# Attention and a gated convolution in one fused kernel: a running sum over all key tiles, a shorter last key tile, 64-row masks, a new order

## The chip, the core and the metric

The kernel runs on one core of a Trainium2 chip. A core has a matrix engine (TensorE; PE in the profile, with its weight loads as PEld), a vector engine (DVE), a scalar engine (ACT), GpSimd (POOL) and a queue engine (SP) that here issues all DMA transfers. Each engine works through its own instructions in the order in which the program lists them; semaphores tie them together. The metric is the time of the whole program on the device, in microseconds; lower is better.

## What is computed

Eight batches of eight attention heads (576 rows, head width 64), and then a feed-forward part on the 512 joined columns:

```python
cum = np.cumsum(np.maximum(s, 0.0), axis=-1)
bias = -(cum[:, :, :, None] - cum[:, :, None, :])
scores = np.where(causal, -1e9, scale * q @ k.T + np.minimum(bias, 0.0))
attn = np.exp(scores - max(scores));  attn = attn / (attn.sum(-1) + 1e-9)
x = attn @ v                                  # heads side by side: 576 x 512
h = np.maximum(x @ w_in, 0.0)                 # 576 x 1024
gate = sigmoid(3-tap convolution of h along the rows)
out = (h * gate) @ w_out                      # 576 x 512
```

## The kernel before

**Attention.** Two heads are handled as one pair, 32 pairs, four to a batch. The two heads of a pair lie in partitions 0 to 63 and 64 to 127, so that their matmuls use 64 rows of the array each and run side by side. Operands are split into a high and a low part. For each pair there are these tasks, with the names that the planner gives them:

- `sh` (line 803): one product of every query row with the keys, in parts for the query tiles 0 to 4 (4 has 64 rows). DVE takes the row maxima from it (`mx`, lines 820 and 825). Tiles 0 to 3 need a causal mask there, which a fused add-and-maximum (line 825) adds; that operation is followed by a read of its accumulator. Tile 4's first part needs none and uses a plain maximum (line 820).
- `tn` (line 841): a 128x128 transpose of the maxima on TensorE; ACT copies the result, a DMA puts it into the operand `eq`.
- `sc` (line 884): the scores transposed, key tile by key tile (448 columns for key tile 1, 320, 192 and, for the last, 64), four steps each; ACT takes the exponential into `pt` (line 906).
- The causal mask of the scores: in the pairs 0 to 8 (`p < B0`) TensorE adds it with a 128x128 bf16 matmul per head and key tile (line 888); later POOL zeroes the triangle in `pt` (line 919).
- `ad` (line 962): from pair 9 on, DVE or POOL add up key tiles 1 (from its second 128 columns on) to 4.
- `sum` (line 997): the sums of the exponentials over the keys, by matmuls with `onehot`. Output row block q (144 columns) of a head goes to one of four groups of 32 columns of the array; the second head uses them in reversed order.
- `pv` (line 944): the product with v, in the same groups of 32 columns.

**Feed-forward.** `h` (line 1094) and `o` (line 1189) are matmuls over the whole array, 1536 each; ACT, DVE and POOL do the convolution, the gate and the split between them (lines 1105 to 1161).

**Order.** Every piece of work is a task with a due time; a planner plays them against assumed durations and writes the program in the order that results. From pair 9 on the tasks of neighbouring pairs stand in one unbroken burst on TensorE:

```python
ORDER = ("sh0", "sh1", "sh2", "sum", "pv", "sc0", "sh3", "sc1", "sc2", "sc3")
```

so that burst p holds `sum` and `pv` of pair p-1, `sc` of p and `sh` of p+1. Feed-forward matmuls and the transpose fill the time between bursts.

## Time and profile before

| | |
|---|---|
| Time, median of 3 runs (lowest to highest) | 812.44 us (810.75 to 814.55) |
| Span of the profiled execution, first to last instruction | 810.0 us |
| TensorE busy | 772.9 us, 95% of the span |
| VectorE busy | 596.5 us, 74% |
| ScalarE busy | 442.1 us, 55% |
| GpSimd busy | 311.6 us, 38% |

The profiled execution lists its span and no time of its own; the runs' median lies 2.4 us above that span. Matmuls are pipelined, so the time from one matmul's start to the next one's is what a matmul costs, not its own duration.

### The profile page before, as it was taken

How to read it: one execution, taken by the hardware profiler on the slowest of the kernel's cores; microseconds unless marked ns; L12 is line 12 of the kernel's file. 1: busy time of each engine (PE TensorE's matmuls, PEld its weight loads, DVE VectorE, ACT ScalarE, POOL GpSimd, SP SyncE). 2: the span in 40 equal slices, each digit the busy share in tenths (PEclk: the TensorE clock that was granted, in tenths of full speed). 3: DMA queues.
4: the chain of work that ended last, by engine and by line, in shares of the span. 5: the costliest groups of instructions: out<-in, count | busy, mean ns of one | idle time of the engine just before them, and what ended most of it. 6: DMA issues, size and time to landing. Idle time of an engine off the chain costs nothing.

```text
span 810.0 us, 21043 instructions
## 1 busy us (share of the span) xinstructions
PE 772.9 (95%) x8371; PEld 693.5 (86%) x8371; DVE 596.5 (74%) x1379; ACT 442.1 (55%) x982; POOL 311.6 (38%) x411
## 2 busy tenths in 40 slices
PE   2699998989999999999999999999999999999998
PEld 2576777779998999999998999999998999998997
DVE  8779778885577778777778778777777778734632
ACT  4364565637455645646555645646455645645633
POOL 7054452433334443443434443543434433422212
PEclk9999999999999999999999999999999999999999
DMA  7355433320213222122213222132213211111001
GB/s 221 122 161 153 134 100 95 120 89 19 82 46 87 77 82 75 46 90 74 82 45 91 73 82 75 46 92 72 83 45 92 72 54 44 44 42 41 16 23 37
DMA packets 49805, 63.24 MB, mean 78 GB/s; under 512 B 5679, under 2 KB 38767, under 8 KB 49647
## 3 DMA queue, kind: packets, MB, share of 16 engines
q1 hardware_dynamic: 49707, 61.91, 25.1%
q8 instruction: 65, 1.06, 0.5%
q14 instruction: 33, 0.27, 0.1%
HBM read 48.60 MB, written 13.04 MB: 76 GB/s over the span
## 4 chain that ended last, share of the span: by engine, by line
PE 87%; DVE 4%; ACT 2%; POOL 2%; DMA 2%; issue 2%; SPq 0%; ACTq 0%; DVEq 0%; POOLq 0%
PE ps L1189 25%; PE ps L1094 25%; PE ps L884 15%; PE pv L944 10%; PE ps L803 6%; PE ps L997 5%; ACT pt L906 1%; DMA ek<-bx 1%; DVE junk L825 1%; DVE ct L1131 1%; PE ps L888 1%; DMA rb<-ri_d 1%; DVE ct L612 0%; ACT s L756 0%; DVE ct L1119 0%
## 5 line engine op out<-in xcount | busy, mean ns | idle before, releaser
L1189 PE MATMUL ps<-u,wo 128*128 128x288 f32 x1536 | 218.0, 299 | 2.0 <-POOL u L1161 1.4
L1161 POOL TENSOR_TENSOR u<-ct,u 128x576 fp32r<-128x576 f32 x64 | 96.7, 1510 | 314.2 <-ACT u L1157 286.2
L1094 PE MATMUL ps<-x,wi 128*128 128x290 f32 x1536 | 215.9, 298 | 0.0
L1189 PEld LDWEIGHTS ps<-u,wo 128*128 128x128 f32 x1536 | 207.6, 188 | 4.7 <-POOL u L1161 1.9
L1094 PEld LDWEIGHTS ps<-x,wi 128*128 128x128 f32 x1536 | 209.1, 190 | 1.1
L906 ACT ACTIVATE pt<-ps,bias_sb 128x288 f32<-128x288 f32 (+4 forms) x384 | 153.5, 477 | 64.7 <-PE ps L884 64.3
L1131 DVE SCALAR_TENSOR_TENSOR ct<-ht,cw_sb,ct 128x288 f32<-128x288 f32 (+1 forms) x256 | 134.3, 525 | 71.7 <-ACT ct L1117 66.8
L825 DVE CUSTOM_DVE_ANT_0 junk<-ps,mask 128x448 bf16<-128x448 f32 (+3 forms) x256 | 108.3, 423 | 27.7 <-PE ps L803 3.5
L884 PE MATMUL ps<-s 64*128 64x288 f32 (+4 forms) x1152 | 125.1, 314 | 3.3 <-DVE r L825 2.5
L884 PEld LDWEIGHTS ps<-s 64*128 64x128 f32 x1152 | 101.7, 189 | 13.0 <-ACT pt L906 5.7
L1105 ACT ACTIVATE ht<-ps 128x289 f32<-128x289 f32 x128 | 52.7, 412 | 83.6 <-PE ps L1094 82.1
L944 PE MATMUL pv<-pt,v 128*32 128x448 f32 (+4 forms) x1536 | 96.0, 395 | 0.0
L919 POOL TENSOR_SCALAR_AFFINE_SELECT pt<-pt 128x128 f32<-128x128 f32 x230 | 67.3, 312 | 73.2 <-ACT pt L906 70.8
L760 POOL TENSOR_TENSOR s<-raw,s 128x1152 fp32r<-128x1152 f32 x31 | 86.5, 2790 | 15.3 <-ACT s L756 9.6
L944 PEld LDWEIGHTS pv<-pt,v 128*32 128x32 f32 x1536 | 54.9, 111 | 38.0 <-issue 29.8
L884 PE MATMUL ps<-eq,ek 64*128 64x288 f32 (+4 forms) x384 | 74.4, 325 | 0.0
L803 PE MATMUL ps<-s 64*128 64x288 f32 (+4 forms) x384 | 66.5, 331 | 6.0 <-DVE r L820 3.2
L1117 ACT ACTIVATE ct<-ht,cw_sb 128x288 f32<-128x288 f32 x126 | 67.7, 537 | 5.8
L1206 ACT COPY ob<-ps 128x288 f32<-128x288 f32 x63 | 25.0, 397 | 80.5 <-PE ps L1189 68.1
L1150 DVE TENSOR_TENSOR ct<-ct,ht 128x576 f32<-128x576 f32 x64 | 54.4, 851 | 16.7 <-ACT ct L1144 16.7
L803 PE MATMUL ps<-ek,eb 64*128 64x288 f32 (+4 forms) x384 | 58.2, 320 | 6.4 <-DMA ek<-bx 6.4
L1144 ACT ACTIVATE ct<-ct 128x576 f32<-128x576 f32 x64 | 43.6, 681 | 31.5 <-DVE ct L1131 31.2
(87 smaller groups left out, 802.8 us busy)
## 6 DMA issues: line engine op xcount, KB each, us to landing
raw<-qk SPq DMA_DIRECT2D x32, 576.0 KB
v<-vp SPq DMA_DIRECT2D x32, 320.0 KB
rb<-ri_d SPq DMA_DIRECT2D x64, 144.0 KB
outT<-ob SPq DMA_DIRECT2D x64, 144.0 KB
ht<-w_out SPq DMA_DIRECT2D x16, 256.0 KB
w<-w_in SPq DMA_DIRECT2D x8, 512.0 KB
ri_d<-ri SPq DMA_DIRECT2D x32, 72.0 KB
rows_d<-bx SPq DMA_DIRECT2D x1, 1215.0 KB
```

The costliest lines, as they stand in the source:

```text
L760: tt_on(e)(st[:, 0:2, :], R_t[raw.slot], st[:, 2:4, :].bitcast(F32), op=ALU.subtract)
L803: nc.tensor.matmul(dst[j], l, m, start=(k == 0), stop=(k == 1))
L825: nc.vector.tensor_tensor_reduce(out=junk[:, 0 : c1 - c0], in0=bank(pb, o, o + c1 - c0), in1=mask[:, S - w + c0 : S - w + c1], scale=1.0, ...
L884: nc.tensor.matmul(dst[j], l, m, start=(k == 0), stop=(k == 3))
L906: nc.scalar.activation(PT_t[pts[j].slot][0:jt, O_T[t] + c0 : O_T[t] + c1], bank(pb, o, o + c1 - c0)[0:jt], AF.Sigmoid, bias=bias_sb[0:jt, ...
L919: nc.gpsimd.affine_select(out=reg, in_=reg, pattern=[[1, dg]], compare_op=ALU.is_ge, fill=0.0, base=0, channel_multiplier=-1,)
L944: nc.tensor.matmul(pvt[gs, o0 : o0 + c1 - c0], vt[0:jt, t, gs], PT_t[pts[g // 2].slot][0:jt, O_T[t] + c0 : O_T[t] + c1], start=(t == 0), s ...
L1094: nc.tensor.matmul(bank(hb, 0, XW), l, r, start=(k == 0), stop=(k == len(seq) - 1))
L1117: nc.scalar.activation(o, src, AF.Copy, scale=w)
L1131: nc.vector.scalar_tensor_tensor(cc[:, lo:hi], h_[:, sh + lo : sh + hi], cw_sb[:, 3 * f + k : 3 * f + k + 1], cc[:, lo:hi], op0=ALU.mult, ...
L1161: tt_on(e)(uu[:, 1], C_t[ct.slot], uu[:, 0].bitcast(F32), op=ALU.subtract)
L1189: nc.tensor.matmul(bank(pb, 0, HS), l, r, start=(fp == 0 and k == 0), stop=(fp == NF // 2 - 1 and k == len(seq) - 1),)
```

## The change

Five things change, and the planner's result with them.

- **Sum.** The running sum now covers all five key tiles: `ad` starts with key tile 1 added to tile 0's columns from 128 on (448 wide), and takes in tiles 2, 3 and 4 as before. The `sum` matmuls read tile 0's first 128 columns and `ad` alone, first all of one head, then all of the other.
- **Last key tile.** Its score matmuls load 66 weight columns where they loaded 128.
- **Early mask.** In pairs 0 to 8 the mask is added by bf16 matmuls of 64 rows and 64 columns, the two heads side by side. It is now also added to `sh`, and DVE takes the plain maximum there for all tiles.
- **Small ones.** The reciprocal is taken in place, the mask operands share `ad`'s memory, and the second pair's `dr` load no longer waits for the first one's in the plan.
- **Order.** The planner's matmul cost is now the larger of streaming and weight load, and every task's due time is shifted by a number from a table (`DUE`, 500 entries; two lines stand here).

```diff
+DUE = {
...
+    "tn":
+        "0 -7.46 2 15.64 3 12.43 4 -45.28 5 9.39 6 3.16 7 29 8 38.87 9 18.73 10 -5.31 11 28.45 "
...
-    unit = const.tile([P, P], BF16, name="unit")
+    unit = const.tile([P, D], BF16, name="unit")
-    ad_t = const.tile([P, 2, W_T[2]], F32, name="ad")
+    ad_t = const.tile([P, 2, W_T[1]], F32, name="ad")
+    mrow = ad_t.bitcast(BF16).rearrange("p a c -> p (a c)")[:, 0 : 4 * P].rearrange(
+        "p (k i m) -> p k i m", k=2, i=2
+    )
...
-        nc.gpsimd.tensor_copy(unit, ident)
+        nc.gpsimd.tensor_tensor(unit, ident[:, 0:D], ident[:, D:P], op=ALU.add)
+        nc.gpsimd.memset(mrow, 0.0)
+        for j in range(2):
+            for i in range(2):
...
-    def c_rt(n):
-        return n * 0.461e-3
+    def c_rt(part, last=P):
+        return sum(max((c1 - c0) / 2.4e3 + 0.013, 0.107 if t < L else last / 1.2e3)
+                   for t, c0, c1 in part)
...
                     for k in range(2):
+                        if k and p < B0 and tau < L:
+                            for i_ in range(0 if tau else 1, 2):
+                                for j, r in enumerate(lanes):
+                                    d0 = c1 - c0 - D * (2 - i_)
+                                    nc.tensor.matmul(
+                                        dst[j][:, d0 : d0 + D], mrow[r, 1, i_], unit[r],
+                                        start=False, stop=False,
+                                    )
...
+                    def plain(tau, c0):
+                        return c0 == 0 and (tau == L or p < B0)
-                        if tau == L and c0 == 0:
+                        if plain(tau, c0):
...
-                    ks = slice(P * t, P * t + P)
-                    dst = [bank(pb, o, o + cn) for pb in pbs]
+                    kn = min(P, J_T[t] + 2)
+                    dst = [bank(pb, o, o + cn)[0:kn] for pb in pbs]
...
-                                l = st[r, kk * S + P * t : kk * S + P * t + P]
+                                l = st[r, kk * S + P * t : kk * S + P * t + kn]
...
                             dg = min(P, cn)
-                            for j in range(2):
-                                nc.tensor.matmul(
-                                    dst[j][:, 0:dg], mask[:, S - P : S], unit[:, 0:dg],
-                                    start=False, stop=False,
-                                )
+                            for i_ in range(dg // D):
+                                for j, r in enumerate(lanes):
+                                    nc.tensor.matmul(
+                                        dst[j][:, D * i_ : D * i_ + D], mrow[r, 0, i_, 0:kn], unit[r],
+                                        start=False, stop=False,
+                                    )
...
-                for t in range(2, NT):
+                for t in range(1, NT):
...
-                            acc, pt[:, O_T[1] + P : O_T[1] + W_T[1]] if t == 2 else acc,
+                            acc, pt[:, P:S] if t == 1 else acc,
                             pt[:, O_T[t] : O_T[t] + W_T[t]], op=ALU.add,
...
                     rows.append([
-                        (0, pt[:, 0:S]), (P, pt[:, O_T[1] : O_T[1] + P]), (2 * P, ad_t[:, j, :])
+                        (0, pt[:, 0:P]), (P, ad_t[:, j, :])
                     ])
...
+            steps = [(i, j) for i in range(n) for j in range(2)]
+            if ad:
+                steps = [(i, j) for j in range(2) for i in range(n)]
...
-            nc.vector.reciprocal(ri_t, rs_t)
+            nc.vector.reciprocal(rs_t, rs_t)
...
+    for t in sch.tasks:
+        t.tag += shift.get(due(t.name), 0.0)
```

What this does to the program shows in the listed order. On TensorE, here is the sum of the fourth burst that has a running sum (pair 12); `pt0` and `pt1` are the two heads' exponentials, `ad` the running sum. Before:

```order
L803 MATMUL ps5_70<-ek2_86,eb_89 128x64
L997 MATMUL ps1_66<-pt0_92,onehot_74 32x144 x4
L997 MATMUL ps1_66<-pt1_93,onehot_74 32x144 x4
L997 MATMUL ps1_66<-pt0_92,onehot_74 32x16
L997 MATMUL ps1_66<-pt0_92,onehot_74 32x112
L997 MATMUL ps1_66<-pt1_93,onehot_74 32x16
L997 MATMUL ps1_66<-pt1_93,onehot_74 32x112
L997 MATMUL ps1_66<-ad_97,onehot_74 32x32
L997 MATMUL ps1_66<-ad_97,onehot_74 32x144 x2
L944 MATMUL pv_64<-pt0_92,v0_90 32x128 x2
```

and the same place after the change:

```order
L934 MATMUL ps5_70<-ek2_86,eb_89 128x64
L1136 MATMUL ps0_65<-pt0_92,onehot_74 32x128
L1136 MATMUL ps0_65<-ad_97,onehot_74 32x16
L1136 MATMUL ps0_65<-ad_97,onehot_74 32x144 x3
L1136 MATMUL ps0_65<-pt1_93,onehot_74 32x128
L1136 MATMUL ps0_65<-ad_97,onehot_74 32x16
L1136 MATMUL ps0_65<-ad_97,onehot_74 32x144 x3
L1082 MATMUL pv_64<-pt0_92,v0_90 32x128 x2
```

Eighteen matmuls became ten (the two `ad` rows of before stand once more, for the second head), and 2048 output columns became 1152. The order is now head by head.

The end of the same burst on TensorE, the last two score matmuls and what follows. Before, six feed-forward matmuls (`u`, `wo`) stand ahead of the transpose of the maxima (`ident`):

```order
L884 MATMUL ps0_65<-eq0_87,ek1_85 128x192
L884 MATMUL ps3_68<-eq0_87,ek1_85 128x192
L1189 MATMUL ps1_66<-u2_977,wo_79 128x288 x6
L841 MATMUL ps2_67<-ident_71,r0_98 128x128
L1189 MATMUL ps1_66<-u3_978,wo_79 128x288 x6
```

After:

```order
L1019 MATMUL ps2_67<-eq0_87,ek1_85 128x192
L1019 MATMUL ps4_69<-eq0_87,ek1_85 128x192
L976 MATMUL ps3_68<-ident_71,r0_98 128x128
L1328 MATMUL ps0_65<-u2_1189,wo_79 128x288 x6
L1328 MATMUL ps0_65<-u3_1190,wo_79 128x288 x6
```

The transpose now stands directly behind the burst. Of the 22 transposes from the first running sum on, that was so for 1 before and is so for 13 now; the others have six or more matmuls in between.

DVE behind that burst, where the running sum of pair 13 is made (`ad`; `ct` is the convolution, `rb` and `x` the normalized output). Before:

```order
L756 CAST s1_83<-raw1_81 128x1152
L962 TENSOR_TENSOR ad_97<-pt0_92 128x320
L1043 TENSOR_TENSOR rb_96<-pv_64,rb_96 128x576
L1058 CAST x_95<-rb_96 128x2x290
L962 TENSOR_TENSOR ad_97<-ad_97,pt0_92 128x64
L1062 TENSOR_TENSOR x_95<-rb_96,x_95 128x2x290
L962 TENSOR_TENSOR ad_97<-pt1_93 128x320
```

After:

```order
L879 CAST s0_82<-raw0_80 128x1152
L1099 TENSOR_TENSOR ad_97<-pt0_92 128x448
L1099 TENSOR_TENSOR ad_97<-ad_97,pt0_92 128x320
L1099 TENSOR_TENSOR ad_97<-pt1_93 128x448
L1099 TENSOR_TENSOR ad_97<-ad_97,pt0_92 128x192
```

The 448-wide add is new, and DVE makes nearly all adds itself: over the program it has 44 of the 46 adds of 448, and 43 of the 46 of 192 where it had 23.

## Rows read from the trace of the kernel before

**Rows 1.** Profile page, its first part: busy time, share of the span, instructions.
```profile
span 810.0 us, 21043 instructions
PE 772.9 (95%) x8371; PEld 693.5 (86%) x8371; DVE 596.5 (74%) x1379; ACT 442.1 (55%) x982; POOL 311.6 (38%) x411
```

**Rows 2.** Busy time by stretch: stretch, length, PE, PEld, DVE, ACT, POOL, clock, DMA.
```profile
25.00:200.00 175.00, 163.71 (x1855) 130.12 (x1854) 141.19 (x357) 95.94 (x221) 65.56 (x45) 0.97 0.36 111
200.00:700.00 500.00, 499.47 (x5572) 458.75 (x5570) 387.37 (x889) 282.38 (x635) 206.78 (x304) 1.00 0.23 70
700.00:810.00 110.00, 104.15 (x917) 99.96 (x917) 48.41 (x91) 54.17 (x114) 24.90 (x34) 0.99 0.11 35
```

**Rows 3.** The chain that ended last, 200 to 700 us, shares by line.
```profile
by line: PE ps L1094 29.0%; PE ps L1189 28.7%; PE ps L884 16.8%; PE pv L944 12.0%; PE ps L803 7.6%; PE ps L997 4.9%; PE ps L841 0.5%; ACT pt L906 0.5%; issue 0.1%; PE ps L888 0.0%
```

**Rows 4.** Timeline of PE in one burst: start, length, engine, line, operation, form, count.
```profile
303.44 0.79 PE L997 MATMUL ps<-pt,onehot 128*32 128x144 f32 x22
304.04 0.29 PE L997 MATMUL ps<-ad,onehot 128*32 128x144 f32 x1
304.06 0.27 PE L997 MATMUL ps<-pt,onehot 128*32 128x112 f32 x2
...
304.41 0.30 PE L944 MATMUL pv<-pt,v 128*32 128x128 f32 x1
...
307.26 0.67 PE L884 MATMUL ps<-s 64*128 64x288 f32 x6
...
307.89 0.31 PE L803 MATMUL ps<-s 64*128 64x320 f32 x2
...
308.39 0.98 PE L884 MATMUL ps<-s 64*128 64x288 f32 x6
...
310.02 0.46 PE L884 MATMUL ps<-s 64*128 64x64 f32 x5
...
310.54 0.53 PE L884 MATMUL ps<-s 64*128 64x320 f32 x4
...
311.73 1.06 PE L1189 MATMUL ps<-u,wo 128*128 128x288 f32 x6
312.63 0.27 PE L841 MATMUL ps<-ident,r 128*128 128x128 f32 x1
```

**Rows 5.** PEld by line and form: count, busy us, mean ns, idle before.
```profile
L884 PEld LDWEIGHTS ps<-s 64*128 64x128 f32 x1152 | 101.7, 189 | 13.0 <-ACT pt L906 5.7 <-DVE r L825 3.6 <-issue 0.5
L944 PEld LDWEIGHTS pv<-pt,v 128*32 128x32 f32 x1536 | 54.9, 111 | 38.0 <-issue 29.8
L888 PEld LDWEIGHTS <-mask 128*128 128x128 bf16 x90 | 5.2, 99 | 7.8 <-issue 6.6
```

**Rows 6.** Timeline of PE, an early pair.
```profile
59.74 1.77 PE L997 MATMUL ps<-pt,onehot 128*32 128x144 f32 x54
61.30 0.30 PE L944 MATMUL pv<-pt,v 128*32 128x128 f32 x2
...
64.19 0.66 PE L884 MATMUL ps<-s 64*128 64x288 f32 x6
...
69.65 0.33 PE L841 MATMUL ps<-ident,r 128*128 128x128 f32 x1
```

**Rows 7.** DVE by line and form, columns as in Rows 5.
```profile
L825 DVE DVE_READ_ACCUMULATOR2_ANT r<- 128x1 f32 x320 | 26.6, 83 | 0.0
L962 DVE TENSOR_TENSOR ad<-pt 128x320 f32<-128x320 f32 x41 | 24.8, 605 | 20.8 <-POOL pt L919 20.8
```

**Rows 8.** Waits, 0 to 200 us: who, for whom, total us, times, longest.
```profile
PEld ps L803 <- DVE r L820: 5.3, 9, 2.0
```

**Rows 9.** Timeline of DVE in the burst of Rows 4.
```profile
311.21 0.08 DVE L825 DVE_READ_ACCUMULATOR2_ANT r<- 128x1 f32 x1
```

**Rows 10.** Timeline of PE, second pair's first products.
```profile
24.58 0.75 PE L803 MATMUL ps<-ek,eb 64*128 64x288 f32 x2 [5.11 <-DMA ek<-bx]
```

More of the change, by code (lines that the diff above doesn't have):

```diff
@@ L3 @@
 import math
+import re
 from contextlib import ExitStack
@@ L60, with due @@
 ORDER = ("sh0", "sh1", "sh2", "sum", "pv", "sc0", "sh3", "sc1", "sc2", "sc3")
+KINDS = {
+    "sh": ("mx",), "tn": ("rt", "ds"), "sc": ("ex", "mk", "ad"), "pv": ("sum",),
+    "nm": ("gd", "inv", "ri", "rb", "xh", "xl"), "g": ("re", "ce", "ta", "ga", "mu", "uh", "ul"),
+    "o": ("oe", "st"),
+}
+DUE = {
+    "x":
+        "s -20.88 masks -12.84 ident -1.96 eb 25.43 cum 47.26 rows_d 1.9 rest 67.91 bias_cp 3.09 "
+        "cw -0.02 cwq 22.44 cwh 8.24",
+    "pads":
+        "0 -16.34 1 15.9 2 -14.42",
+    "ind":
[78 rows of a table added]
+}
+def due(name):
+    kind, rest = re.match(r"([a-z]+)(.*)", name).groups()
+    if not rest or kind in ("bias", "rows"):
+        return "x:" + name
+    for of, kinds in KINDS.items():
+        if kind in kinds:
+            kind = of
+    n = 2 if kind in ("h", "g", "o", "wo") else 1
+    return kind + ":" + ".".join(re.findall(r"^[\d.]*", rest)[0].split(".")[:n])
 class Buf:
@@ L350 @@
     cw_sb = const.tile([P, NF * 3], F32, name="cw_sb")
-    junk = const.tile([P, S], BF16, name="junk")
+    junk = const.tile([P, W_T[1]], BF16, name="junk")
     wi = const.tile([P, 2, NC, DF], F32R, name="wi")
@@ L371 @@
     rs_t = const.tile([P, RS], F32, name="rs")
-    ri_t = const.tile([P, RS], F32, name="ri")
     H_t = [const.tile([P, 2, XW], F32, name=f"ht{i}") for i in range(NHT)]
@@ L806, in pair @@
             w = sum(c1 - c0 for _, c0, c1 in part)
-            t_mm = add(f"sh{p}.{i}", [("PE", 2 * c_rt(w))], [t_hi, t_dr, t_eb],
+            t_mm = add(f"sh{p}.{i}", [("PE", 2 * c_rt([(0, *x[1:]) for x in part]) + (0 if p >= B0 else 0.06 * sum(2 if tau else 1 for tau, _, _ in part if tau < L)))],
+                       [t_hi, t_dr, t_eb, t_ident],
                        a_sh + 0.1 * i, sh_mm, alloc=pbs + ([r8] if i == 0 else []),
@@ L832, in pair @@
                     maxima.append(
-                        add(f"mx{p}.{j}.{tau}.{c0}", [("DVE", (0.15 if tau == L and c0 == 0 else 0.22) + (c1 - c0) / 0.96e3)],
+                        add(f"mx{p}.{j}.{tau}.{c0}", [("DVE", (0.15 if plain(tau, c0) else 0.22) + (c1 - c0) / 0.96e3)],
                             [t_mm, t_ident] + ([maxima[j]] if c0 else []), a_sh + 0.1 * i,
@@ L886, in sc_mm @@
                             dg = min(P, cn)
[L887 to L891 removed]
+                            for i_ in range(dg // D):
[3 more added lines that the diff above has]
+                                        start=False, stop=False,
+                                    )
                     o += cn
             w = sum(c1 - c0 for _, c0, c1 in part)
[L895 removed]
+            t_sc = add(f"sc{p}.{i}", [("PE", 4 * c_rt(part, 66) + (0 if p >= B0 else 0.06 * sum(-(-min(P, c1 - c0) // D) for _, c0, c1 in part if c0 == 0)))], [t_ident, t_shift, t_lo], A + 0.1 * i,
                        sc_mm, alloc=pbs + (pts if i == 0 else []), uses=[sb, ek, eq], mode="r",
@@ L969, in pair @@
                         f"ad{p}.{j}.{t}", [("DVE", c_tt(w), True, ADD_), ("POOL", c_pool(w), True, ADP)],
-                        [m for t_, m in masks[j] if t_ in (1, t)] + [t_ad], A + 2, pre_add,
-                        alloc=[ad] if (j, t) == (0, 2) else [], uses=[*pts] + ([] if (j, t) == (0, 2) else [ad]),
+                        [m for t_, m in masks[j] if t_ in (t - (t == 1), t)] + [t_ad] + last_mask, A + 2, pre_add,
+                        alloc=[ad] if (j, t) == (0, 1) else [], uses=[*pts] + ([] if (j, t) == (0, 1) else [ad]),
                     )
@@ L986, in sums @@
             n = len(rows[0])
-            for i in range(n):
-                for j in range(2):
-                    c0, src = rows[j][i]
-                    c1 = c0 + src.shape[1]
-                    for q in range(c0 // RS, 4):
-                        g = 3 - q if j else q
-                        a_, b_ = max(c0, q * RS), min(c1, (q + 1) * RS)
-                        if a_ >= b_:
-                            continue
-                        o0 = a_ - q * RS
-                        nc.tensor.matmul(
-                            bank(sb_, o0, o0 + b_ - a_)[32 * g : 32 * g + 32], onehot[:, j, :],
-                            src[:, a_ - c0 : b_ - c0], start=i == 0 and j == 0,
-                            stop=i == n - 1, tile_position=(0, 32 * g),
-                            skip_group_check=True,
-                        )
+            steps = [(i, j) for i in range(n) for j in range(2)]
+            if ad:
+                steps = [(i, j) for j in range(2) for i in range(n)]
+            for i, j in steps:
+                c0, src = rows[j][i]
+                c1 = c0 + src.shape[1]
+                for q in range(c0 // RS, 4):
+                    g = 3 - q if j else q
+                    a_, b_ = max(c0, q * RS), min(c1, (q + 1) * RS)
+                    if a_ >= b_:
+                        continue
+                    o0 = a_ - q * RS
+                    nc.tensor.matmul(
+                        bank(sb_, o0, o0 + b_ - a_)[32 * g : 32 * g + 32], onehot[:, j, :],
+                        src[:, a_ - c0 : b_ - c0], start=j == 0 and (i == 0 or (ad is not None and q > 0)),
+                        stop=j == 1 if ad else i == n - 1, tile_position=(0, 32 * g),
+                        skip_group_check=True,
+                    )
         ta = A1 + 1
         tq = ta - TQA
-        t_sum = add(f"sum{p}", [("PE", 1.0 if ad else 1.4)], [t_ident] + added + [m for t, m in masks[0] + masks[1]], tq, sums,
+        t_sum = add(f"sum{p}", [("PE", 0.6 if ad else 1.4)], [t_ident] + added + [m for t, m in masks[0] + masks[1]], tq, sums,
                     alloc=[sb_], uses=[*pts] + ([ad] if ad else []), mode="c32", burst=group(p + 1))
@@ L1238, in stay_awake @@
         )
+    shift = {
+        f"{kind}:{n}": float(v)
+        for kind, text in DUE.items() for n, v in zip(text.split()[::2], text.split()[1::2])
+    }
+    for t in sch.tasks:
+        t.tag += shift.get(due(t.name), 0.0)
     order = sch.play(
```

22 lines of the change are left out of this document (16 added, 6 removed), and 76 rows, old and new, of the table DUE.

## The prediction

> **What bounds the kernel now.** I read the page first: over 810.0 us TensorE is busy for 95%, the next engine, DVE, for 74% [rows 1]. A share is an average over stages, so the stretches come next. From 25 to 200 us TensorE works 163.7 of 175 us; from 200 to 700 us it works 499.5 of 500; in the last 110 us 104.2 [rows 2]. The chain says the same for the middle: 99.4% of it lies on seven matmul lines, 0.5% on ScalarE [rows 3]. The reader is to see that in these 500 us nothing but matmul time counts: what TensorE is spared there comes off the span, as long as no other engine then makes it wait. DVE is the one to watch: 387.4 of 500 us [rows 2]. Before 200 us TensorE is idle for 11.3 us, and waits there are mostly for DVE's row maxima: one line's weight loads wait 5.3 us for them [rows 8].
>
> **The sum.** One sum of before starts at 303.44 and the next task at 304.41: 0.97 us [rows 4]. Per head, tile 0 fills output columns 0 to 575, tile 1 128 to 255, `ad` 256 to 575. Counted over both heads (the second uses the groups in reversed order), the middle two of the four column groups carry 144+144+112+32+144 = 576 columns, the outer two 448. If the groups run side by side, a column costs 0.97/576 = 1.68 ns. The early sums check it: 800 columns in every group, 1.56 us [rows 6], 1.95 ns a column with many short pieces. After the change every group carries 288 columns: two blocks of 144, or 128+16 and 144. That gives 0.48 to 0.56 us; I take 0.50, since there are few short pieces. Saving 0.47 x 23 pairs = **10.8 us**. Bounds: nothing (first rival) to 11.3.
>
> Whether groups run side by side decides this, and the trace shows it. At 304.04 a matmul of `ad` starts, before the two 112-column ones of tile 1 that start at 304.06 and stand ahead of it in the program for either head [rows 4]. So a group goes on while another is behind. The Trainium skill, page "TensorE: Matmul & The Clock Gate", Part 3, "The mechanism", says the opposite: matmuls start and end strictly in program order, only weight loads are pulled ahead. By that rule the new order, 128 and 16 columns into one group ahead of the other three, would save nothing here (the first rival's 803.4 us). The trace contradicts it; the measurement decides.
>
> **The last key tile.** Its eight matmuls start at 310.02 and the next tile's last lane at 310.54, where 64 columns of streaming cannot be what takes 0.13 us a step: the weight loads are [rows 4]. A load of 128 columns shows 189 ns, one of 32 shows 111: 0.81 ns a column [rows 5]. 62 columns fewer are 50 ns. Of four loads the first lies under the 448-wide matmul before it, so three count (the two heads load side by side): 0.15 us a pair, x 32 = **4.8 us**. Bounds: 0 to 4 x 0.05 x 32 = 6.4.
>
> **The early mask.** A masked pair's scores take from 64.19 to 69.65, 5.46 us [rows 6]; an unmasked one's 307.26 to 307.89 and 308.39 to 311.73, 3.97 us [rows 4]. So ten full-array mask matmuls, with the array's tiling changed ten times, cost 1.49 us. They go. In come 9 steps of two 64-row matmuls in `sc` (two for each of four tiles, one for the last) and 7 in `sh`. No row has such a step. Below, 64 columns at the full clock are 27 ns; above, a step that waits for a whole fp32 weight load costs the 0.13 us just seen. The mask's bf16 loads are short, 99 ns against 189 [rows 5], so I stay near the low end: 0.05. Per pair -1.49 + 16 x 0.05 = -0.69, x 9 = **6.2 us** saved. Bounds: 16 x 0.13 = 2.08 would cost 5.3; 0.03 would save 9.1.
>
> DVE's maxima of the early pairs lose 72 accumulator reads (320 to 248 in the listed program) of 83 ns [rows 7], 6.0 us of DVE work; the plain maximum itself I cost like the fused one. It counts only where TensorE waits for maxima, at least the 5.3 us of [rows 8]; I take a third, **2 us**. Bounds 0 and 6.
>
> **More work for the running sum.** 46 adds of 448 columns: 320 take 605 ns [rows 7], so 0.6 to 0.85 us, near 0.75. DVE also takes over 20 adds of 192 from POOL. About 45 us more, less some casts and splits it hands to ACT and POOL. Spread over the middle stretch that is 387 + 40 of 485 us, 88%. It lies beside the matmuls and is costed at nothing there. Queued behind it on DVE are the convolution taps, which feed the gate, and the next maxima; the sum itself waits for the second head's last add. With the cover gone, each add that falls on the path would cost its 0.6 to 0.85 us.
>
> **The order.** Outside the early masks the array's tiling changes 146 times, 137 before, counted in the listed programs. A change costs at most 1.49/10 = 0.15 us, since the mask matmuls share that: **+1.4 us**, 0 as the other bound. 13 transposes now stand directly behind their burst. In the burst shown DVE's last maximum ended at 311.29 [rows 9], the burst at 311.73, and six matmuls of 0.90 us covered the rest before 312.63 [rows 4]. The burst gets 0.47 + 0.15 = 0.62 us shorter, so the maxima, if they end as they did, are 0.18 us late at a transpose without cover: **+2.6 us** for 13 with the 0.2 I take. What is behind a late transpose is the `eq` transfer for the next burst's scores, a whole stretch of feed-forward matmuls away.
>
> **The start.** The second pair's products waited 5.11 us, until 24.58, for their bias rows [rows 10]. That transfer now stands ahead of two 576 KB loads instead of behind one; but POOL first builds eight more mask pieces, ahead of the padding that this transfer waits for, and the first weight pieces stand on DVE between the second pair's maxima. I take zero, from -3 to +5 (the wait gone by half, or as long again). The in-place reciprocal, smaller tiles and the dropped plan edge are nothing: the buffer was already held until the spread was done.
>
> **Sum.** -10.8 - 4.8 - 6.2 - 2.0 + 1.4 + 2.6 = -19.8. From the span of 810.0 that is 790.2 us; the runs' median lies 2.4 above the span, and I leave that: **792.6 us**.
>
> **Rivals.**
>
> 1. *The sums do not speed up*, because a group's work blocks the others in the queue. Per head 144 columns in the outer group, then 144 in the others: 288 x 1.68 ns = 0.48, two heads 0.97, as now. For it: the new order puts four passes of one group first. Against: the starts at 304.04 and 304.06 [rows 4]. Time 792.6 + 10.8 = 803.4 us. Chance 0.07.
>
> 2. *Late maxima take the place of the removed work, and it gets slower.* Place: the transposes behind the burst, and the burst's own `sh` banks, which DVE must empty. Price: every 0.1 us by which DVE is later costs 2.2 us over 22 bursts. For it: DVE goes from 77% towards 88% in the middle, and the plan's durations only have to be wrong by a few per cent. Against: DVE still has 12% to spare, and before the plan met its marks to 0.5 us in 500. With 0.7 us more a burst it is 792.6 + 15.4 = 808.0; slower than before by over 0.5% it is from (816.5 - 792.6)/22 = 1.1 us a burst on, one and a half of the new adds in each. Chance of a loss of 0.5 us or more a burst 0.12, a quarter of it beyond 1.1.
>
> 3. *The early part gains nothing or loses*: the new mask steps cost as fp32 loads, the start takes 5 us more, the clock (granted at 0.97 there [rows 2]) drops once or twice more. 792.6 + 6.2 + 5.3 = 804.1 with the mask at its bound. Chance 0.09.
>
> The change not doing what it says would need 66 columns to load as slowly as 128: 797.4, inside the range.
>
> **Numbers.** The forecast, that TensorE's removed time comes off, has 0.72 (its own range 783 to 800); 0.07, 0.12 and 0.09 go to the rivals. To hold 8 in 10 the range takes in the first and most of the third rival: **782 to 804**. A measurement of this kernel can hardly tell a change under 0.5%, 4 us, from none. Faster by more than that (under 808.4): 0.72 + 0.07 + 0.09 + half of the second rival = 0.93, rounded to 0.92; within 0.5%: 0.04; slower: 0.04.
>
> **What would show it.** Right: a sum of about 0.5 us between `sh` and `pv` in the middle, and 23 of them; the last key tile's eight matmuls in about 0.37 us; an early pair's scores near 4.4 us; TensorE still over 99% busy in the middle stretch, which ends some 16 us earlier. Wrong: sums near 0.97 us; idle time ahead of the transpose with DVE's maximum named; waits for `ad`; a first score matmul later than before. The prediction fails if the middle is no longer all matmul time.

## The result, and the profile after

The changed kernel takes 789.5 us (median of four runs, 788.2 to 791.3) where the kernel before took 812.9 beside it: a ratio of 0.972, 95% interval 0.969 to 0.974. The prediction was 792.6 us, 782 to 804. The profiled execution's span fell from 810.0 to 788.0 us, by 22.0 where the sum of the terms said 19.8.

The page's first part and the middle stretch (columns as in [rows 1, 2]):

```profile
PE 744.9 (95%) x8201; PEld 669.6 (85%) x8201; DVE 595.3 (76%) x1375; ACT 439.2 (56%) x972; POOL 323.4 (41%) x408
```
```profile
200.00:700.00 500.00, 494.86 (x5324) 447.11 (x5317) 399.08 (x958) 288.70 (x645) 218.45 (x310) 1.00 0.23 70
```

TensorE's busy time fell by 28 us, the span by 22. The middle is no longer all matmul time: 494.9 of 500 us, where it was 499.5. The chain of 200 to 700 us says so as well; DVE and ScalarE stand on it now, against 0.5% of ScalarE alone in [rows 3]:

```profile
by line: PE ps L1233 27.9%; PE ps L1328 27.5%; PE ps L1019 16.6%; PE pv L1082 11.4%; PE ps L934 6.8%; PE ps L1136 2.7%; DVE ad L1099 1.1%; DVE ct L1270 1.1%; issue 0.9%; DVE junk L960 0.9%; PE ps L976 0.8%; DVE r L955 0.6%; ACT pt L1044 0.5
```

The timeline of TensorE in the burst of [rows 4], which now stands 12.4 us earlier:

```profile
291.00 0.30 PE L1136 MATMUL ps<-pt,onehot 128*32 128x128 f32 x1
291.01 0.32 PE L1136 MATMUL ps<-ad,onehot 128*32 128x144 f32 x3
...
291.57 2.87 PE L1082 MATMUL pv<-pt,v 128*32 128x128 f32 x48
...
296.93 0.31 PE L1019 MATMUL ps<-s 64*66 64x64 f32 x3
...
297.34 0.53 PE L1019 MATMUL ps<-s 64*128 64x320 f32 x4
...
298.51 0.33 PE L976 MATMUL ps<-ident,r 128*128 128x128 f32 x1
298.60 1.83 PE L1328 MATMUL ps<-u,wo 128*128 128x288 f32 x12
```

The sum takes 0.57 us (291.00 to 291.57) where it took 0.97; the last key tile 0.41 (296.93 to 297.34) where it took 0.52; the transpose behind the burst 0.09 until the next matmul. An `ad` matmul starts 0.01 us behind the 128-column one of another group. The early pair of [rows 6], in the same view:

```profile
61.65 0.23 PE L923 MATMUL ps<-unit,ad 64*128 64x64 bf16 x4
61.72 0.34 PE L934 MATMUL ps<-ek,eb 64*128 64x192 f32 x2
61.89 0.59 PE L1019 MATMUL ps<-s 64*128 64x288 f32 x6
...
66.21 0.33 PE L976 MATMUL ps<-ident,r 128*128 128x128 f32 x1
```

Four mask matmuls, two steps, take 0.07 us (61.65 to 61.72), so a step is 0.035. The masked scores run from 61.89 to 66.21, 4.32 us, where they took 5.46. The weight loads, which answer to [rows 5], and the adds, to [rows 7] (count, total us, mean ns):

```profile
L1019 PEld LDWEIGHTS ps<-s 64*128 64x128 f32 x960 | 85.0, 188 | 16.8 <-DVE r L955 5.5 <-ACT pt L1044 4.4 <-DVE r L960 0.9
L1019 PEld LDWEIGHTS ps<-s 64*66 64x66 f32 x192 | 15.7, 135 | 0.7
```
```profile
L1099 DVE TENSOR_TENSOR ad<-pt 128x448 f32<-128x448 f32 x44 | 36.4, 834 | 16.5 <-POOL pt L1057 16.4
```

To see which task lost and which gained, I added up TensorE's timeline, for each task from its first start to the next task's first start, so that a wait counts with the task ahead of it. Early runs from TensorE's first matmul (13.0 us before, 11.6 after) to the first sum that uses the running sum; rest runs from there to the start of the last `o` matmuls, 16.8 us before the end in both. The masks of `sh` stand under mask, and tasks that hardly changed have no column; us:

| | early | sc | mask | sh | pv, tn | rest | sum | sc | sh | h, o | 
|---|---|---|---|---|---|---|---|---|---|---|
| before | 227.1 | 53.0 | 9.7 | 42.6 | 36.3 | 553.0 | 22.5 | 85.1 | 37.9 | 341.6 |
| after | 213.0 | 42.9 | 7.3 | 47.1 | 31.7 | 546.7 | 13.1 | 83.6 | 42.0 | 342.2 |

In the rest 9.4 us of sum time went and 6.3 us of them are left: the `sh` products, whose matmuls are the same, take 4.1 us more, because TensorE waits inside the bursts. Before, all 21 full bursts took 9.50 to 9.61 us; after, 9 of them take 8.8 to 8.9 and the other 12 take 9.1 to 10.9.

### The profile page after: what moved, and what is told of

It is laid out like the page before. It is cut to its first block, busy times and chain, and to the rows that moved or that the text cites. A ratio compares the mean times of both kernels' runs of the same rounds, so it can differ in the third digit from the quotient of the medians.

```text
span 788.0 us, 20648 instructions
## 1 busy us (share of the span) xinstructions
PE 744.9 (95%) x8201; PEld 669.6 (85%) x8201; DVE 595.3 (76%) x1375; ACT 439.2 (56%) x972; POOL 323.4 (41%) x408
## 4 chain that ended last, share of the span: by engine, by line
PE 82%; DVE 6%; ACT 2%; issue 2%; DMA 1%; POOL 1%; DVEq 0%; SPq 0%; ACTq 0%; POOLq 0%
PE ps L1233 25%; PE ps L1328 24%; PE ps L1019 13%; PE pv L1082 9%; PE ps L934 6%; PE ps L1136 3%; DVE ct L1270 2%; ACT pt L1044 1%; DVE r L955 1%; DVE ad L1099 1%; DVE junk L960 1%; PE ps L976 1%; DMA rb<-ri_d 1%; POOL u L1300 0%; DMA ht<-w_out 0%
## 5 line engine op out<-in xcount | busy, mean ns | idle before, releaser
L1270 DVE SCALAR_TENSOR_TENSOR ct<-ht,cw_sb,ct 128x288 f32<-128x288 f32 (+1 forms) x256 | 137.9, 545 | 51.2 <-ACT ct L1256 46.3
L1019 PE MATMUL ps<-s 64*128 64x288 f32 (+4 forms) x1152 | 120.6, 307 | 7.8 <-DVE r L955 5.3
L1057 POOL TENSOR_SCALAR_AFFINE_SELECT pt<-pt 128x128 f32<-128x128 f32 x230 | 79.4, 369 | 99.7 <-ACT pt L1044 96.9
L1019 PEld LDWEIGHTS ps<-s 64*128 64x128 f32 (+1 forms) x1152 | 97.1, 179 | 17.4 <-DVE r L955 5.5
L883 POOL TENSOR_TENSOR s<-raw,s 128x1152 fp32r<-128x1152 f32 x32 | 89.5, 2797 | 39.2 <-ACT s L879 28.7
L960 DVE CUSTOM_DVE_ANT_0 junk<-ps,mask 128x64 bf16<-128x64 f32 (+3 forms) x184 | 77.1, 419 | 16.7 <-PE ps L934 3.8
L1082 PEld LDWEIGHTS pv<-pt,v 128*32 128x32 f32 x1536 | 51.3, 111 | 40.2 <-issue 29.9
L934 PE MATMUL ps<-s 64*128 64x288 f32 (+4 forms) x384 | 65.3, 329 | 11.4 <-DVE r L955 5.7
L1099 DVE TENSOR_TENSOR ad<-ad,pt 128x192 f32<-128x192 f32 (+2 forms) x132 | 68.6, 556 | 6.4 <-POOL pt L1057 6.3
L1256 ACT ACTIVATE ct<-ht,cw_sb 128x288 f32<-128x288 f32 x122 | 65.1, 536 | 4.7
L955 DVE TENSOR_REDUCE r<-ps 128x1 f32<-128x288 f32 (+4 forms) x136 | 52.3, 431 | 19.7 <-PE ps L934 18.3
L1289 DVE TENSOR_TENSOR ct<-ct,ht 128x576 f32<-128x576 f32 x64 | 53.7, 839 | 13.2 <-ACT ct L1283 12.4
```

The lines of the kernel that those rows point to most:

```text
L883: tt_on(e)(st[:, 0:2, :], R_t[raw.slot], st[:, 2:4, :].bitcast(F32), op=ALU.subtract)
L934: nc.tensor.matmul(dst[j], l, m, start=(k == 0), stop=(k == 1))
L960: nc.vector.tensor_tensor_reduce(out=junk[:, 0 : c1 - c0], in0=bank(pb, o, o + c1 - c0), in1=mask[:, S - w + c0 : S - w + c1], scale=1.0, ...
L1019: nc.tensor.matmul(dst[j], l, m, start=(k == 0), stop=(k == 3))
L1057: nc.gpsimd.affine_select(out=reg, in_=reg, pattern=[[1, dg]], compare_op=ALU.is_ge, fill=0.0, base=0, channel_multiplier=-1,)
L1082: nc.tensor.matmul(pvt[gs, o0 : o0 + c1 - c0], vt[0:jt, t, gs], PT_t[pts[g // 2].slot][0:jt, O_T[t] + c0 : O_T[t] + c1], start=(t == 0), s ...
```

## The experiments

Times are medians; each ratio is to the kernel before on the same chip (0.972 for the changed kernel).

| kernel | us | ratio, 95% interval | span |
|---|---|---|---|
| sum_old | 800.1 | 0.988 (0.984 to 0.992) | 797.5 |
| last128 | 797.3 | 0.984 (0.981 to 0.986) | 795.0 |
| mask_full | 801.7 | 0.989 (0.986 to 0.992) | 800.4 |
| sh_fused | 795.7 | 0.981 (0.979 to 0.984) | 789.0 |
| order0 | 812.7 | 1.002 (1.000 to 1.004) | 809.4 |
| old_order | 803.0 | 0.991 (0.988 to 0.994) | 796.6 |
| old_work | 811.0 | 0.999 (0.997 to 1.002) | 809.7 |
| fewer_adds | 790.6 | 0.974 (0.968 to 0.979) | 790.4 |
| mx_first | 828.4 | 1.021 (1.018 to 1.025) | 822.0 |
| mx_inv | 792.3 | 0.976 (0.973 to 0.980) | 793.1 |
| sum_groups | 788.9 | 0.973 (0.969 to 0.976) | 787.4 |
| late_w | 794.0 | 0.979 (0.975 to 0.982) | 790.3 |

The changed kernel, `sum_old`, `fewer_adds` and `sum_groups` are the same program up to the first running sum, and reached it between 224.0 and 229.1 us in their profiled executions: what the clock does at the start (last section) moves a span by up to 5 us. So below I also give what a kernel gains or loses from that sum on.

### One part undone at a time

The sum's matmuls of before:

```diff
-                        (0, pt[:, 0:P]), (P, ad_t[:, j, :])
+                        (0, pt[:, 0:S]), (P, pt[:, O_T[1] : O_T[1] + P]),
+                        (2 * P, ad_t[:, j, P:])
...
-                steps = [(i, j) for j in range(2) for i in range(n)]
```

> The changed kernel, whose sum matmuls read tile 0, tile 1's first 128 columns and the running sum from its 128th column on, in the old order (18 matmuls, 2048 columns for 10 and 1152); adds and plan stay, and so tile 0 is counted twice in the columns from 256 on and the columns 128 to 255 lack tiles 2 to 4. Theory (a sum costs what its fullest column group streams, and comes off the path): sums back at 0.97 us, 789.5 + 23 x 0.40 = 798.7 us. Rival (the bursts are held by DVE or by the semaphores, so that the sums' time is hidden): under 793 us.

800.1 us, as the theory said. From the first running sum to the last, 22 sums, it falls 6.5 us behind the changed kernel, where 22 x 0.40 would be 8.8: the scores got 2.5 us shorter, since part of the sum's time covers waits behind it. The sum of one burst in its timeline (294.47 to 295.44):

```profile
294.47 0.79 PE L1135 MATMUL ps<-pt,onehot 128*32 128x144 f32 x22
...
295.44 0.30 PE L1082 MATMUL pv<-pt,v 128*32 128x128 f32 x1
```

128 weight columns:

```diff
-                    kn = min(P, J_T[t] + 2)
+                    kn = P
```

> The changed kernel with 128 instead of 66 weight columns in the last key tile's score matmuls. Theory (three of the four weight loads per pair show): 789.5 + 32 x 0.11 = 793.0 us, the eight matmuls of that tile in 0.52 us instead of 0.41. Rival (hidden behind the waits for banks): 789.5 us.

797.3 us, more than either. Behind the first running sum it loses 3.3 us over 22 bursts, 0.15 each, where the theory had 0.11; the eight matmuls take 0.55 us in this burst (301.16 to 301.71). The other 3.7 us of its span arose ahead of that sum. Nine pairs of 0.15 make 1.4 of them; the rest fits the clock, which after its first rise fell back to its lower level for 17.1 us there, against 10.2 in the changed kernel.

```profile
301.16 0.49 PE L1019 MATMUL ps<-s 64*128 64x64 f32 x5
...
301.71 0.54 PE L1019 MATMUL ps<-s 64*128 64x320 f32 x4
```

The full-array score mask (`eye` is a bf16 identity):

```diff
-                            for i_ in range(dg // D):
-                                for j, r in enumerate(lanes):
...
+                            for j in range(2):
+                                nc.tensor.matmul(
+                                    dst[j][:, 0:dg], mask[:, S - P : S - P + kn], eye[:, 0:dg],
```

> The changed kernel whose score mask in the pairs 0 to 8 is again a 128x128 matmul over the whole array per head and key tile (ten per pair, the array's tiling changed ten times); the masks of sh stay as changed. Theory (TensorE sets the early part's time too): the ten cost 1.49 us where 9 steps of 0.035 us stood, 789.5 + 9 x 1.2 = 800 us. Rival (the early part waits for the row maxima, the exponentials and the start anyway): at most 793 us.

801.7 us. The masked scores of a pair take 5.59 us again, 66.47 to 72.06, against 4.32. All of the lag is there at the first running sum (12.28 us) and stays to the last (12.33): it is made in the pairs 0 to 8 and nothing later gives it back. 9 x 1.27 are 11.4; but the first sum, 5.1 us late, still ran at the lower clock level, so part of the 12.3 is the clock's. At three later sums in a row, pairs 5 to 7, it is 8.75, 10.05 and 11.32 us behind, so that a pair does lose about 1.27 us there. The timeline shows where a full-array step costs: 0.21 us from the two mask matmuls' start to the next product.

```profile
66.47 0.58 PE L1021 MATMUL ps<-s 64*128 64x288 f32 x6
66.98 0.29 PE L1025 MATMUL ps<-ad,mask 128*128 128x128 bf16 x2
67.19 0.40 PE L1021 MATMUL ps<-eq,ek 64*128 64x288 f32 x2
...
72.06 0.33 PE L978 MATMUL ps<-ident,r 128*128 128x128 f32 x1
```

No mask in `sh`, fused maxima:

```diff
-                        if k and p < B0 and tau < L:
+                        if False:
...
-                        return c0 == 0 and (tau == L or p < B0)
+                        return c0 == 0 and tau == L
```

> The changed kernel without the masks on TensorE in the sh products of the pairs 0 to 8; VectorE takes the fused add-and-maximum with its accumulator read there, as before; everything else and the order stay. TensorE has 9 x 7 steps less (63 x 0.035 = 2.2 us), VectorE 72 reads of 83 ns more (6.0 us). Theory (my third of the reads, 2 us, is hidden in the waits, so both cancel): 788.5 to 790.5 us. Rival 1 (TensorE's steps are the price): 787 us. Rival 2 (VectorE's maxima set the early part): 793 us or more.

Inconclusive. The profiled execution (790.7 us, the lowest of five) loses 0.9 us ahead of the first running sum and nothing behind it; the other four took 794.5 to 797.6. By the profile both sides cancel, by the median rival 2 is right, and what the clock does at the start moves a time by as much. What the early maxima's reads are worth, and the TensorE steps against them, stays open.

### What the order is worth

The table off:

```diff
-        t.tag += shift.get(due(t.name), 0.0)
+        t.tag += 0.0
```

> The changed kernel with every shift of the due-time table set to zero; all other edits stay. Theory (the time comes from TensorE work that is gone: sums, last key tile, masks): the plain order costs little, 790 to 797 us, and the sum still takes 0.57 us in the middle. Rival (the new order brings most of the 23 us): 800 us or more, with TensorE idle for 10 us more in the middle.

812.7 us: my theory fell. The sums take 0.57 us, and yet all is lost again. TensorE has 17 us of idle time in the middle, where the changed kernel has 5, and `sh` takes 53.4 us of the rest instead of 42.0. Its waits from 226 to 720 us name DVE's maxima:

```profile
PE ps L1136 <- DVE r L955: 12.5, 6, 2.7
```

It is the sum behind the `sh` products that waits, 2.7 us in each of four bursts. In the first of them six taps of the convolution stand ahead of a maximum on DVE, then a gate product and two more taps:

```profile
361.50 3.03 DVE L1270 SCALAR_TENSOR_TENSOR ct<-ht,cw_sb,ct 128x288 f32<-128x288 f32 x6
...
366.09 0.82 DVE L955 TENSOR_REDUCE r<-ps 128x1 f32<-128x288 f32 x2
```
```profile
366.69 0.27 PE L1136 MATMUL ps<-pt,onehot 128*32 128x128 f32 x1 [2.67 <-DVE r L955]
```

Is the new order worth all, or is this one just bad? Two more kernels fill a table. The new work in the order of before (the planner gets its old costs, tasks and due times; the engines' lists are the same task by task, and the two first adds stand together):

```diff
-        return sum(max((c1 - c0) / 2.4e3 + 0.013, 0.107 if t < L else last / 1.2e3)
+        return n * 0.461e-3
...
+                        if t == 2:
+                            tt_on(e)(
+                                ad_t[:, j], pt[:, P:S], pt[:, O_T[1] : O_T[1] + W_T[1]], op=ALU.add,
+                            )
```

> The changed kernel's matmuls, masks, adds and maxima in exactly the order in which the planner put the kernel before (its costs, its due times, no table; the 448-wide add stands directly ahead of the 320-wide one of the same task). Theory (the TensorE work that is gone comes off the span in any order that was fitted once, and the changed kernel without its table was slow because that order was fitted to nothing): about 9.2 + 3.5 + 9 off 812, 790 to 796 us. Rival (shorter TensorE work and longer DVE work need a new order, without which the row maxima come late in each burst as they did without the table, 0.5 us a burst): 803 us or more, with the sh products of the later part at 48 us or more instead of 38.

Between the two: 803.0 us (798.4 to 808.4; the profiled one is the lowest). And the work of before in the new order: `sum_old`, `last128`, `mask_full` and `sh_fused` together, and no 448-wide add.

> The changed kernel's order with all the work of before: 18 sum matmuls, 320-wide first add (the 448-wide one is gone, its place in the order empty), 128 weight columns, full-array score masks, no mask in sh and the fused maxima everywhere. With the three others it fills a table of old and new work in old and new order (spans: old work, old order 810.0; new work, old order 796.6; new work, new order 788.0). Theory (the order was fitted to the new work; by itself it brings nothing): 808 to 816 us. Rival (the new order is better for any work, by the 8.6 us that it brings with the new work): 801 to 804 us.

| median us (span) | old order | new order |
|---|---|---|
| old work | 810 to 813 (810.0) | 811.0 (809.7) |
| new work | 803.0 (796.6) | 789.5 (788.0) |

The new order brings nothing to the old work. The new work brings 7 us in the old order by the ratio (0.991), 13 by the spans; together they bring 23 and 22. So the order is worth 9 us by the spans, 14 by the medians and 16 by the ratios, with this work alone. Part of that goes through TensorE's clock: its granted mean is 0.985 to 0.989 in the ten runs of `old_order` and 0.991 to 0.995 in the four of the changed kernel. What the nine slower runs lost against the profiled one stands in no trace. In the profiled executions `old_order` needs 547.4 us for the rest, as much as the changed kernel (546.7): its bursts all take 9.25 to 9.36 us, 0.2 to 0.35 less than before, because at their end the scores' weight loads wait for DVE's maxima (27 waits, 7.0 us):

```profile
PEld ps L1017 <- DVE r L958: 7.0, 27, 0.4
```

The new order has many bursts of 8.8 us and a few bad ones instead, and is ahead in the early part, 213.0 us against 220.5 (transposes 4.7 for 8.8, masks 7.3 for 9.9, scores 42.9 for 45.7; `sh` goes the other way, 47.1 for 42.7). There too the clock has a part: it fell back to its lower level for 17.1 us in `old_order` and for 10.2 in the changed kernel, which can make at most half the difference, 3.4 us.

### Is VectorE too slow, or in the wrong place?

The adds of tiles 2 to 4 left out:

```diff
+                        if t > 1:
+                            return
```

> The changed kernel in its own order, with the running sum ended after its first add (the adds of key tiles 2 to 4 are left out, and so are these tiles in the sums): DVE has some 70 us less to do, spread over the middle. Theory (DVE is late with the row maxima because of the adds, which costs about 0.2 us a burst in the sh products, and 5 us of idle time in the middle): 781 to 785 us, sh products of the later part at 38 us instead of 42. Rival (the waits come from where the maxima stand in the order, the DVE has room enough): 787 to 790 us, sh at 41 us or more.

The rival: 790.6 us, although DVE works 540 us instead of 595. Behind the first running sum it gains 2.0 us, 1.8 of them in `sh`. One burst, which falls from 10.39 to 8.82 us, makes 1.6 of the 2.0: in the changed kernel two adds take 4.75 us together there, the maxima behind them come late, and the sum waits.

```profile
415.62 4.75 DVE L1099 TENSOR_TENSOR ad<-pt 128x448 f32<-128x448 f32 x2
```
```profile
423.38 0.30 PE L1136 MATMUL ps<-pt,onehot 128*32 128x128 f32 x1 [1.25 <-DVE r L955]
```

In the other bad bursts what holds TensorE may then be where DVE's work stands. The worst of them, 10.9 us, in the changed kernel, first DVE, then TensorE:

```profile
582.66 0.51 DVE L960 CUSTOM_DVE_ANT_0 junk<-ps,mask,r 128x288 bf16<-128x288 f32 x1
...
583.10 0.75 DVE L1289 TENSOR_TENSOR ct<-ct,ht 128x576 f32<-128x576 f32 x1
583.77 1.06 DVE L1270 SCALAR_TENSOR_TENSOR ct<-ht,cw_sb,ct 128x287 f32<-128x287 f32 x2
584.75 1.05 DVE L1160 RECIPROCAL rs<-rs 128x144 f32<-128x144 f32 x1
585.72 0.42 DVE L960 CUSTOM_DVE_ANT_0 junk<-ps,mask,r 128x288 bf16<-128x288 f32 x1
```
```profile
588.00 0.42 PE L934 MATMUL ps<-s 64*128 64x320 f32 x2 [0.65 <-ACT pt L1044]
...
589.89 0.87 PE L1019 MATMUL ps<-s 64*128 64x448 f32 x6 [0.59 <-ACT pt L1044]
```

Gate products, taps and a reciprocal stand between two maxima. In the trace of before, four such operations stand between the first and the last maximum of every burst; after, one to four in the nine short bursts and two to seven in the twelve long ones, five or more in six of these. So I let the maxima pass them, on DVE alone, where their products are done by then in the plan:

```diff
+            if not is_mx(m) or x.name[:2] not in ("ta", "mu", "uh", "hi", "in"):
+                continue
...
+            if sh.start + sh.opts[0][1] > x.start + 0.4:
+                continue
...
+                order[a : c + 1] = go + [t for t in order[a:c] if t not in go]
```

> The changed kernel with VectorE's order alone altered from pair 10 on: a row maximum whose products the plan has done by then (or within 0.4 us) goes ahead of the convolution taps, gate products, reciprocals and casts that stand before it. Theory (the bursts of 9.2 to 10.9 us, against 8.8 us, are those in which up to five such operations stand between the maxima and TensorE waits for the banks): the sh products of the later part go from 42.0 towards 39 us, 785.5 to 788 us. Rival (the taps are then late for the feed-forward matmuls, which give it back, or the banks wait for ScalarE's exponentials): 789 to 792 us.

828.4 us, far worse than the rival. The scores of the rest take 104.7 us instead of 83.6. A burst of it, ScalarE, then TensorE:

```profile
607.73 0.89 ACT L1044 ACTIVATE pt<-ps,bias_sb 128x288 f32<-128x288 f32 x2
610.09 0.68 ACT L1283 ACTIVATE ct<-ct 128x576 f32<-128x576 f32 x1 [1.47 <-DVE ct L1270]
610.68 0.88 ACT L1044 ACTIVATE pt<-ps,bias_sb 128x288 f32<-128x288 f32 x2
```
```profile
611.21 1.49 PE L1019 MATMUL ps<-s 64*128 64x448 f32 x6 [1.62 <-ACT pt L1044]
```

ScalarE works in order: its gate (L1283) stands between two groups of exponentials and waits 1.47 us for the taps, which now come behind the maxima on DVE. The next exponentials wait behind the gate, their bank stays full, and TensorE waits 1.62 us. After it the 448-wide products run 1.49 us where they took 0.87: from 612.4 to 616.0 the granted clock is 0.50, the lower level, in the second of these rows of the stretches:

```profile
226.00:745.00 519.00, 492.30 (x5136) 443.87 (x5125) 393.44 (x929) 279.17 (x625) 210.08 (x298) 0.97 0.22 65
...
612.40:616.00 3.60, 3.60 (x31) 3.25 (x30) 1.12 (x3) 2.28 (x6) 2.63 (x5) 0.50 0.21 64
```

So the loss has two parts. From 226 to 745 us TensorE is idle for 26.7 us (5.7 from 226 to 720 us in the changed kernel), and the clock, 0.97 on average there against 1.00, stands at its lower level for 27.3 us in all, which can cost up to 13.7 us; together that is about the 33 us by which the rest is longer.

ScalarE's waits for the taps are 44.9 us in this kernel and 19.3 in the changed one. To test it, only the reciprocals and casts are passed (`("in", "hi")` in the list above):

> As the kernel that put the row maxima first, but only reciprocals and casts are passed; convolution taps and gate products keep their place ahead of the maxima. Theory (the 34 us lost there came from the taps: ScalarE's gate stands in its order ahead of the exponentials and waits for the taps, so the exponentials come late and TensorE's score matmuls wait for their banks): nothing of that loss, the score products of the later part near 83.6 us instead of 104.7, and 786 to 791 us. Rival (TensorE lost the time because VectorE's maxima, now early in its order, waited for their products and held everything behind them): a loss in proportion to the moved operations, 795 us or more.

The scores are at 84.1 us, all of the loss is gone, and the rest takes 547.3 us, as in the changed kernel. The six times are 789.7 to 790.7 and 794.0 to 794.9, three each; the profiled one is of the upper three, and its lag is there from the first sums (2.9 us at the first, 4.7 in the middle, 5.1 at the end), ahead of anything that was altered. So the taps held the loss. Only a dozen operations were passed here, most of them reciprocals, and that brings nothing; what it would bring if the maxima passed the taps and the gate held nothing up is not shown.

### Two attempts at more

The 16 columns that share a group with the 128 go last:

```diff
-                for q in range(c0 // RS, 4):
+                for q in sorted(range(c0 // RS, 4), key=lambda q: (q == 0) if ad else q):
```

> The changed kernel with the sum's matmuls in another order: per head the 128 columns of tile 0, the three 144-wide ones of the other groups, and only then the 16 columns that go to the same group as the 128. Theory (a column group that is still busy holds up those behind it in the listed order, only some matmuls deep): the sum goes from 0.571 us towards 0.50, 23 x 0.05 to 0.07 = 1 to 2 us off 789.5. Rival (each group's own columns set it, whatever the order): 0.57 us as before, 789.5 us.

The sum goes to 0.52 us (290.35 to 290.87), as the theory said, and the time stays: 546.7 us for the rest, as before it; 0.8 us less of sums, 0.8 more of waits in `pv`, `sc` and `sh` behind them.

```profile
290.35 0.30 PE L1136 MATMUL ps<-pt,onehot 128*32 128x128 f32 x1
...
290.87 0.28 PE L1082 MATMUL pv<-pt,v 128*32 128x128 f32 x2
290.88 0.18 PE L1136 MATMUL ps<-ad,onehot 128*32 128x16 f32 x1
```

The first weight pieces behind the second pair's maxima:

```diff
+    late = [t for t in order if t.name in ("wi11", "wi12", "wi01")]
+    last = next(i for i, t in enumerate(order) if t.name == "mx1.1.1.0")
```

> The changed kernel, on DVE at the start alone: the three operations on the first two loaded weight pieces that stood between the second pair's row maxima, and waited there for their DMA, now stand behind the last of these maxima. Theory (they hold up the first scores at 31.5 us): the first score matmul starts 3 to 5 us earlier, of which 1 to 4 us are left at the end, 785.5 to 788.5 us. Rival (the planes of the weights are then late, or the next wait takes its place): 789 to 791 us.

The first scores start at 27.00 instead of 31.52 us, and then wait 2.27 us for `eq` and 1.56 for exponentials; 794.0 us. The next waits took its place, and the clock was later: the first sum takes 2.60 us (43.21 to 45.81), so that most of it still ran at the lower level, where the changed kernel's takes 1.56 (40.53 to 42.09). What the earlier scores would be worth at the changed kernel's clock is not shown.

```profile
30.38 0.61 PE L1019 MATMUL ps<-eq,ek 64*128 64x288 f32 x2 [2.27 <-DMA eq<-rt]
...
33.51 0.74 PE L1019 MATMUL ps<-s 64*128 64x448 f32 x2 [1.56 <-ACT pt L1044]
```

None of the kernels is measurably faster than the changed one.

## Why the prediction held, step by step

**The sum**, -10.8 predicted: 23 x 0.40 = -9.2, of which `sum_old` finds 6.5 to 7 on the path. The groups run side by side, as [rows 4] had shown, and the first rival is out (0.57 us, not 0.97). The Trainium skill, "TensorE: Matmul & The Clock Gate", Part 3, "The mechanism", has matmuls start in strict program order; the starts at 290.87 and 290.88 above contradict that. My 0.50 was too good because the order of the list does count a little: with the 16 columns last it is 0.52.

**The last key tile**, -4.8: -3.5 by the two timelines (0.11 x 32), -4.8 by `last128` (0.15 x 32). 66 columns load in 135 ns, where 189 less 50 is 139. So two to three of a pair's four loads show, and the term held.

**The early mask**, -6.2: the scores lose 5.46 - 4.32 = 1.14 us a pair, 0.11 of it the last tile's, and `sh` has seven steps of 0.035 more. 9 x (1.03 - 0.25) = -7.0; with the 1.27 of `mask_full` it is -9.2. A step is nearer to the low bound than I took it.

**DVE's reads**, -2.0: open, as `sh_fused` could not tell.

**The order**, +1.4 + 2.6 + 0 at the start: the step that was wrong in kind. The 13 transposes cost 0.09 us each, no late maximum behind the burst is seen there, and I had taken the order for a small loss. The table of orders shows that it is the condition of about half the gain. What I had feared at the transposes came inside the bursts: `sh` +4.1 us, 0.18 a burst, a quarter of the 0.7 us of the second rival. My reason for it was at most half right. DVE's load is not it, but for one burst (`fewer_adds`: 2.0 us for 55 us less work). That the place of its taps and gate products can hold TensorE, directly or through ScalarE's order, `order0` and `mx_first` show; that it makes the rest of the changed kernel's own 4.1 us is likely and not shown, as no kernel here got them back.

**The start**, put at zero: both things that I had weighed there happened. The second pair's products wait 1.81 us, until 21.31, instead of 5.11; then the first scores wait 5.29 us for DVE's maxima, because an operation on a weight piece stands between these and waits 4.89 us for its DMA. They start at 31.52 instead of 28.89, the later first score matmul that I had named as a sign of being wrong; in before, though, only one matmul ran at 28.89 and the others at 31.00. First before, then after:

```profile
28.89 0.60 PE L884 MATMUL ps<-s 64*128 64x288 f32 x1 [0.29 <-DVE r L825]
31.00 1.09 PE L884 MATMUL ps<-s 64*128 64x288 f32 x5 [1.51 <-DVE r L825]
```
```profile
31.52 1.09 PE L1019 MATMUL ps<-s 64*128 64x288 f32 x6 [5.29 <-DVE r L955]
```
```profile
29.04 0.43 DVE L733 TENSOR_SCALAR w<-w 128x512 uint32<-128x512 uint32 x1 [4.89 <-DMA w<-w_in]
```

**The middle at over 99% busy**: it is 98.97%. By the last line of the prediction its mechanism failed there in part: 5 us of the middle are idle, which I had put at nothing. What "busy" hid before: the last 40 score products of a burst took 3.25 to 3.36 us in 16 of the 21 bursts of before and 3.0 in the other five, with the same matmuls. 21 weight loads waited up to 0.3 us each for exponentials, under matmuls that still ran, and the share stood at 99.9%. So there was some cover in a middle that I had read as pure matmul time.

**DVE's adds**: 834 ns on average, where I had 0.75 us; but 40 of the 44 take 0.61 to 0.71 us, and the other four 1.4, 1.6, 3.4 and 4.2. What held those four was not found. On the path are the 2.0 us above, mostly the burst of the longest one.

The measured terms, -9.2 - 3.5 - 7.0 + 4.1, make -15.6 of the span's -22.0, and -19.1 with the prices of `last128` and `mask_full`. At the first sum the changed kernel is 4.4 us ahead already: its clock was up there, that of before was not yet (its first sum takes 2.71 us). Some of the first masks is in these 4.4 too, so they cannot simply be added; what is left stays in the open terms. That the total met the forecast so closely owes something to errors of both signs, and to a clock at the start that the forecast did not have. One sum of the prediction is off: 0.72 + 0.07 + 0.09 and half of 0.12 make 0.94, not 0.93.

## What to carry to other kernels

Work taken off the bounding engine came off the time in full only in an order that was planned for it, and 7 to 13 of 22 us in the old one; measure the edit and the order apart, and both together. An engine with 20% to spare can still hold the bound, through the place of one operation in another engine's order: follow the chain past the engine that the wait names, in `mx_first` from TensorE's bank to the exponential, the gate ahead of it and the tap on VectorE. A mean of many operations can hide a few long ones, as with the adds. And a part that takes the same time in every repetition need not be at its floor.

## What the hardware showed

- **The clock's first rise.** In the changed kernel's profile four mask matmuls take 0.14 us at 32.41 and 0.07 at 34.88, twice as fast: TensorE went from the lower to the higher level between them. The first sum takes 1.56 us there (40.53 to 42.09). In `mx_inv`, which is the same program in the pairs 0 to 8, the first sum takes 2.92 us (43.46 to 46.38): it still ran at the lower level. At the fifth sum (98.41 and 101.83) the two executions of one program are 3.4 us apart by that. From 123.3 to 126.5 us the granted clock is 0.50 in `mx_inv` and 1.00 in the changed kernel, and at the first running sum they are 4.5 us apart (224.58 and 229.12). That fits the two groups of its times, though only one of the six has a trace. What decides when the rise comes was not found.

```profile
32.41 0.33 PE L1024 MATMUL ps<-unit,ad 64*128 64x64 bf16 x4
32.55 0.59 PE L1019 MATMUL ps<-eq,ek 64*128 64x288 f32 x2
...
34.88 0.23 PE L1024 MATMUL ps<-unit,ad 64*128 64x64 bf16 x4
34.95 0.45 PE L1019 MATMUL ps<-eq,ek 64*128 64x448 f32 x2
```
```profile
43.46 3.23 PE L1136 MATMUL ps<-pt,onehot 128*32 128x144 f32 x54
46.38 0.43 PE L1082 MATMUL pv<-pt,v 128*32 128x128 f32 x2
```

- **Groups of 32 columns.** A matmul of the next task starts ahead of one that is listed before it and waits for its group: at 290.87 `pv` before the 16-column `ad` at 290.88. In all 23 sums of `sum_groups` it is so, by 0.01 to 0.02 us.
